# Attention with a gated feed-forward: x stored first and the gated tiles added to it in memory, first loads by SyncE, a new order of tasks

## The chip, the cores and the metric

The kernel runs on one core of a Trainium2 chip. The metric is device microseconds for one launch. A core has TensorE (PE in the profile, its weight loads PEld), VectorE (DVE), ScalarE (ACT), GpSimd (POOL) and SyncE (SP). Each runs its own list of instructions in order, and waits on semaphores for the others. Transfers are issued from SP's queue or from POOL's queue. All transfers share 16 DMA engines.

## The reference

Two stages follow one another. In the code below B is 4, H is 8, S is 768 and D is 64; heads 0, 2 and 6 attend to everything before them, the others only to the first 4 keys and to a window of 64.

```python
scores = scale * np.matmul(q, k.transpose(0, 1, 3, 2))
scores = np.where(mask, scores, -1e9)
a = np.exp(scores - max); a = a / (a.sum(-1) + 1e-9)
x = np.matmul(a, v).transpose(0, 2, 1, 3).reshape(3072, 512)

g, val = x @ w_gate, x @ w_val            # 512 -> 1536
ffn_out = (0.5 * g * (1 + erf(g / sqrt(2))) * val) @ w_out
out = x + sigmoid(x @ w_res) * ffn_out    # 3072 x 512, float32
```

## The kernel before

**Tiling.** The 3072 rows are cut into six chunks of 512 rows, four tiles of 128 each (`CHUNKS`, L25). The code numbers the chunks from 0; this text does too, so "from chunk 2 on" in the change's short name is `c >= 1`. For each chunk the kernel does attention, which leaves x for the 512 rows in `xtok` (128 x 4 x 512, f32, two buffers) and, transposed in f16, in `xT`; then `gate_value` (twelve blocks `f`, each with four matmuls of 512 columns for the gate and four for the value, a GELU on ACT and a product on DVE, L1166 and L1168); then the output.

**Output.** Chunk 0's first two tiles use plain matmuls (`output`, L1295). All other pairs of tiles use seven products in place of eight, on sums of halves (`output_fast`, L1212): `keep` copies a partial product out of PSUM, `plus` (L1257) adds another to it, `gated` (L1281) multiplies by `1 + tanh(res / 2)`, whose matmuls are `res`, and `add` (L1286) adds x from `xtok`. SP then stores the finished tile `otile` (128 x 512 f32, four buffers, L1292). For the last pair the adds go by half tiles, and each may go to DVE or POOL.

**Loads.** POOL issues all loads of queries, keys, values and weights (L577); each converts f32 in memory to f16 on the chip. Chunks 0 and 1 load rows of q and k and transpose them on PE (`loads_rows`, L709). Later chunks load tiles (`loads_natural`) and SP issues transposing transfers (L754) into `qkt`. For every batch, SP also copies one pair of heads of `qkt` to other partitions (`q6`, L762) and values shifted by half a tile (`vs`, L662). PE's score matmuls (L893) read `qkt` and `q6`; the weighted values (L516, L1017) read `va` and `vs`.

**Order.** `Graph.schedule` (L219) places every task once, at build time, on its engine's list. A task has a priority; the string `HINTS` (L46) overrides 171 of them by number. The planner's own estimates of each task (`c_act`, `c_dve`, and so on) decide which task is free next. What comes out is five fixed lists. Before the first gate block `g0` is placed, PE's idle time is filled with matmuls on zeros (`warm`, L1333). Each transfer has a semaphore, and SP's last instructions wait for all transfers named `out`.

**Shapes on PE.** A score matmul uses half of the rows of PE's array, the sink scores (L984) a quarter of the columns; the transposes and the window products use half of the columns; the rest uses the whole array, or from about chunk 3 on pairs of half-column matmuls (L517), so that less changes from one shape to the next.

Of the kernel before, what the change touches and what calls it, by code (L numbers as in the profile page):

```python
# [4 lines left out]
NHEAD = 8  # L5
# [15 lines left out]
AF = mybir.ActivationFunctionType  # L21
ALU = mybir.AluOpType
# [21 lines left out]


HINTS = (  # L46
    "3:-58.9 11:-130.04 428:854.14 430:718.61 444:2782.08 457:-821.9 460:407.45 490:4205.68 521:1522.06 "
    "591:-818.43 610:-36.63 612:486.89 613:-2965.25 619:1544.03 621:-44.07 643:467.87 644:-881 646:4.3 656:119.6 "
    "664:25.04 673:629.62 675:-109.25 695:-2674.26 696:-1856.67 703:-881.5 706:-108.75 707:714.39 708:1939.7 "
    "711:270.02 712:497.18 716:476.22 720:652.56 738:638.32 743:520.23 744:3053.24 749:514.3 750:1799.28 "  # L50
    "751:2383.53 756:521.28 762:1469.72 764:4344.87 767:2237.74 787:-603.93 815:5053.25 817:2978.67 821:1231.87 "
    "824:1484.86 836:2402.62 837:798.1 841:706.04 848:-288.52 849:2997.07 876:2751.74 906:2555.54 913:1516.93 "
    "918:2437.99 919:1519.88 924:1537.25 931:1510.23 936:2384.32 949:2443.79 955:2089.28 967:2846.74 995:-227.38 "
    "1001:29.83 1002:3171.86 1003:3180.29 1004:1146.58 1007:2686.58 1012:1781.89 1040:-803.29 1043:1907.45 "
    "1045:1028.83 1046:667.33 1050:3229.28 1051:1536.45 1053:3573.03 1056:-1823.77 1084:4090.27 1110:2454.97 "
    "1111:2597.62 1117:2808.38 1123:2507.5 1128:2481.58 1129:2529.63 1134:2508.5 1146:2434.73 1152:2779.33 "
    "1153:3034.61 1158:3861.94 1165:2795.06 1171:3076.63 1176:2997.8 1185:5989.69 1188:2243.92 1189:2528.84 "
    "1192:2789.39 1193:2537.45 1194:3836.22 1208:3021.15 1215:6294.68 1263:3219.13 1268:5037.38 1283:4420.5 "
    "1308:4756.92 1311:3513.6 1317:3517.03 1321:3052.3 1329:5930.49 1330:3507.5 1335:3508.5 1336:3519.22 "
    "1341:4624.14 1345:3444.6 1353:3516.64 1354:3538.83 1357:2761.66 1365:3787.63 1366:5173.04 1372:5102.72 "  # L60
    "1386:5438.32 1392:4014.31 1393:4933.66 1418:5146.68 1430:4133.91 1441:5428.8 1452:5127.54 1457:2188.42 "
    "1462:4595.33 1464:5711.23 1467:9389.54 1468:4425.54 ~1471:550.69 1476:5611.77 1499:4504.13 1513:6742.83 "
    "1516:5340.27 1522:4510.5 1523:4585.63 1526:3632.38 1534:4503.02 1539:4253.34 1550:4463.64 1565:7711.51 "
    "1570:4506.5 1571:5085.34 1580:2427.42 1594:2466.44 1610:9272.71 1625:3048.93 1627:6036.71 1629:6167.81 "
    "1631:5064.12 1644:6476.5 1662:4125.72 1671:5044.95 1672:7314.6 1676:4967.2 1683:6427.71 1692:9540.12 "
    "1711:7387.16 1757:5137.62 1784:5507.1 1797:5469.41 1803:7562.23 1817:7773.49 1818:7478.69 1823:7672.83 "
    "1834:7419.08 1836:10250.4 1849:7490.55 "
)

class Task:  # L70
# [118 lines left out]
SWAP = -3000.0  # L189
VK_AT = -18.5  # L190
VS_DMA = 0
LAT = {"pe": 0.20, "act": 0.10, "dve": 0.08, "pool": 0.12, "sp": 0.1}


class Graph:
# [205 lines left out]
    def emit(self):  # L401
        nc = self.nc
        sems = {e: nc.alloc_semaphore(f"cnt_{e}") for e in ENGS}
        val, groups = {}, {}
        for e in ENGS:
            n = 0
            for t in self.prog[e]:
                if t.dma:
                    key = (t.eng, t.grp) if t.grp is not None else t.seq
                    if key not in groups:  # L410
                        groups[key] = [nc.alloc_semaphore(f"dma_{t.seq}"), 0]
                    t.sem = groups[key][0]
                    groups[key][1] += 16
                    val[t] = key
                else:
                    n += 1 if t.signal else 0
                    t.sem = sems[e]
                    val[t] = n

        def run(name, engine):  # L420
            for t in self.prog[name]:
                for sem, v in dict.fromkeys((w.sem, groups[val[w]][1] if w.dma else val[w]) for w in t.waits):
                    engine.wait_ge(sem, v)
                self.run = t.run
                res = t.fn(engine)
                last = res[-1] if isinstance(res, (list, tuple)) else res
                if t.dma:
                    last.then_inc(t.sem, 16)
                elif t.signal:
                    last.then_inc(t.sem, 1)  # L430

        finals = [t for t in self.order_ if t.dma and t.name.startswith("out")]
        with nc.Block() as blk:

            @blk.gpsimd
            def _(e):
                run("pool", e)

            @blk.tensor
            def _(e):  # L440
                run("pe", e)

            @blk.scalar
            def _(e):
                run("act", e)

            @blk.vector
            def _(e):
                run("dve", e)

            @blk.sync
            def _(e):
                run("sp", e)
                for t in finals:
                    e.wait_ge(t.sem, 16)


def c_mm(n, k=1):
# [1 line left out]


def c_act(n):
    return 0.19 + n * 0.000834


def c_dve(n, rate=1.0, psum=True):
    return (0.125 if psum else 0.065) + n * 0.00104 / rate


def c_pool(n, rate=1.0):  # L470
# [3 lines left out]
def build_kernel(nc, q, k, v, w_gate, w_val, w_out, w_res, out):  # L474
    assert N_SINK <= 64 and WINDOW == 64
    G = Graph(nc)
# [195 lines left out]
    def loads_rows(c, si, b, a, z):  # L672

        n = z - a
        BB = batch(b)
# [11 lines left out]
        def piece(j, h, i):  # L687
            o = h * 256 if c == 0 else (j * NHEAD + h) * 128
            return at(st[j])[:, o + i * 64:o + (i + 1) * 64]
        for gi, (h0, h1) in enumerate(groups):  # L690
            for j, src in enumerate((q, k)):
                t = dma("pool", base + 4 * gi + j, (h1 - h0) * n * (0.092 if c else 0.089),
                        (lambda j=j, h0=h0, h1=h1: lambda: sv(j, h0, h1, n * 64))(),
                        src[b, h0:h1, lo:hi, :].rearrange("h (p j) d -> p h (j d)", j=n), bufs=[st[j]])
                t.late = 1.2 if c else 0.0
                for h in range(h0, h1):
                    tok[j, h] = t
        values(b, a, z, base + (10 if c == 0 else 2), False, c == 0)
# [33 lines left out]
    def loads_natural(c, si, b, a, z):  # L732
# [8 lines left out]
        for i in range(a, z):  # L741
            for j, src in ((1, k), (0, q)):
                st = sts[(i - a) // 2]

                def sv(i=i, j=j, st=st):
                    o = (j * 2 + (i - a) % 2) * 512
                    return at(st)[:, o:o + 512]
                ds = [dma("pool", base, 0.45,
                          (lambda sv=sv, o=o: lambda: sv().rearrange("p (o h d) -> p o h d", o=2, h=4)[:, o, :, :])(),
                          src[b, :, i * 128:(i + 1) * 128, :].rearrange("(h o) p d -> o p h d", o=2)[o], bufs=[st],  # L750
                          grp=("ld", b, i, j)) for o in range(2)]
                for d in ds:
                    d.late = 5.0
                t = G.add("sp", 1.65, (lambda sv=sv, i=i, j=j: lambda e: e.dma_start(  # L754
                    at(BB.qkt)[:, j, :, i * 128:(i + 1) * 128], sv(), transpose=True))(), ds, base, bufs=[st, BB.qkt], dma=0.85, name="dT")
                t.late = 1.0
                loaded.append(t)
                for p in range(NPAIR):
                    (BB.ktok if j else BB.qtok)[p, i] = t
            if i == a:  # L760
                values(b, a, z, base, False)
# [437 lines left out]
    def weight_sums():  # L1199
# [9 lines left out]
        add(2, w(1, 1), w(0, 1), tall)  # L1209
        add(3, w(1, 0), wt[:, 1], [t2])  # L1210

    def output_fast(c, pi, h, htoks, hs, stoks, xbuf, xtoks, xtbuf, xttoks):  # L1212
        segs = [(b, t) for (b, a, z) in CHUNKS[c] for t in range(a, z)]
        lts = (2 * pi, 2 * pi + 1)
# [57 lines left out]
        for i, lt in enumerate(lts):  # L1272
# [6 lines left out]
            for w, src, deps in parts:  # L1279
                n = w.stop - w.start  # L1280
                ends.append(G.add("dve", c_dve(n, 1.0, src is not None), (lambda w=w, src=src, ot=ot, sr=sr: lambda e: e.scalar_tensor_tensor(  # L1281
                    out=at(ot)[:, w], in0=at(sr)[:, w], scalar=1.0, in1=at(src or ot)[:, w], op0=ALU.add, op1=ALU.mult))(),
                    [tas[i]] + deps, pr + (len(ends) - 40 if end else 0), bufs=[sr, ot] + ([src] if src else []), name="gated"))
            adds = []
            for w, deps in [(p[0], [t_]) for p, t_ in zip(parts, ends)] if end else [(slice(0, 512), ends)]:
                fn = (lambda ot=ot, lt=lt, w=w: lambda e: e.tensor_tensor(  # L1286
# [57 lines left out]
    for c, segs in enumerate(CHUNKS):  # L1344
# [7 lines left out]
                xttoks.extend(halves[-1])  # L1352
        else:
            attention(c, segs, xbuf, xtbuf, xtoks, xttoks)
        h, htoks = gate_value(c, xtbuf, xttoks, halves)
        if c == 0:
            weight_sums()
# [87 lines left out]
```

The softmax here doesn't subtract the row's maximum and nothing guards it: scores larger than these inputs give would overflow.

## Time and profile before

| what | value |
|---|---|
| time, median of 3 runs (lowest to highest) | 266.18 us (265.86 to 267.08) |
| profiled execution, span | 263.7 us |
| median less span | 2.5 us |
| PE busy | 257.7 us, 98% of the span |
| DVE / ACT / POOL busy | 181.6 / 147.2 / 89.3 us |
| DVE adding x (L1286), full tiles | 21 instructions, 14.3 us in all |
| stores of output tiles (256 KB each) | 22, median 2.4 us from issue to landing |
| bytes read from / written to HBM | 29.36 / 6.29 MB |

The profiled execution's own time is its span; no other time is given for it. The span counts from the first to the last instruction of the program, and the 2.5 us are what lies around it.

In the profile, `out<-in` names what an instruction writes and reads, `xN` says how many like it are merged, and square brackets or the last columns give the engine's idle time before it and what ended that. The view of stretches gives, per stretch, its length and for each engine the busy time and the number of instructions. The chain of waits goes back from the last instruction to what released each step. For a transfer, "to landing" runs from its issue to the semaphore's last count.

### The profile page before, as it was taken

How to read it: one execution, taken by the hardware profiler on the slowest of the kernel's cores; microseconds unless marked ns; L12 is line 12 of the kernel's file. 1: busy time of each engine (PE TensorE's matmuls, PEld its weight loads, DVE VectorE, ACT ScalarE, POOL GpSimd, SP SyncE). 2: the span in 40 equal slices, each digit the busy share in tenths (PEclk: the TensorE clock that was granted, in tenths of full speed). 3: DMA queues.
4: the chain of work that ended last, by engine and by line, in shares of the span. 5: the costliest groups of instructions: out<-in, count | busy, mean ns of one | idle time of the engine just before them, and what ended most of it. 6: DMA issues, size and time to landing. Idle time of an engine off the chain costs nothing.

```text
span 263.7 us, 7495 instructions
## 1 busy us (share of the span) xinstructions
PE 257.7 (98%) x3226; PEld 164.0 (62%) x3226; DVE 181.6 (69%) x378; ACT 147.2 (56%) x237; POOL 89.3 (34%) x127
## 2 busy tenths in 40 slices
PE   7999999999999999999999999999999999999993
PEld 6777655468444668544567444589655588655692
DVE  2698437798447888557898366888557689837655
ACT  2785467974244987423787242967243888233430
POOL 8999979506109973975000000000000000000003
PEclk9999999999999999999999999999999999999999
DMA  6999999999999999999996110004200004200003
GB/s 83 174 204 206 188 175 231 175 153 204 134 200 148 165 137 177 171 179 176 174 156 150 42 40 0 2 26 101 82 2 0 2 2 122 82 2 0 2 35 127
DMA packets 96513, 29.22 MB, mean 111 GB/s; under 512 B 84449, under 2 KB 93025, under 8 KB 96481
## 3 DMA queue, kind: packets, MB, share of 16 engines
q0 software_dynamic: 70320, 14.69, 67.5%
q1 hardware_dynamic: 26160, 14.07, 28.0%
q8 instruction: 25, 0.41, 0.7%
q14 instruction: 8, 0.06, 0.1%
HBM read 29.36 MB, written 6.29 MB: 135 GB/s over the span
## 4 chain that ended last, share of the span: by engine, by line
PE 95%; DMA 2%; DVE 1%; issue 0%; POOLq 0%
PE ps L516 50%; PE ps L517 32%; PE ps L893 5%; PE ps L1333 2%; PE ps L1017 2%; PE ps L709 2%; DMA qks<-in_q_dram 2%; PE ps L1106 2%; PE ps L984 1%; DVE otile L1281 1%; DVE otile L1286 1%; DVE otile L1257 0%; POOLq L1427 0%
## 5 line engine op out<-in xcount | busy, mean ns | idle before, releaser
L1166 ACT ACTIVATE gact<-ps 128x512 f16<-128x512 f32 x68 | 40.2, 597 | 73.5 <-PE ps L516 43.7
L1168 DVE SCALAR_TENSOR_TENSOR hT<-gact,ps 128x512 f16<-128x512 f16 x68 | 46.1, 686 | 48.0 <-PE ps L516 23.1
L516 PE MATMUL ps<-xT,wg 128*128 128x512 f16 (+1 forms) x208 | 50.0, 363 | 0.0
L516 PE MATMUL ps<-xT,wv 128*128 128x512 f16 (+1 forms) x202 | 49.0, 362 | 0.0
L1286 POOL TENSOR_TENSOR otile<-otile,xtok 128x256 f32<-128x256 f32 x3 | 2.4, 801 | 136.2 <-DVE otile L1281 136.2
L577 POOL DMA_DIRECT2D qks<-in_k_dram x36 | 28.0, 810 | 17.3 <-DMA qkt<-qks 13.9
L516 PEld LDWEIGHTS ps<-xT,wg 128*128 128x128 f16 x208 | 20.1, 98 | 20.0 <-DVE otile L1257 0.3
L516 PEld LDWEIGHTS ps<-xT,wv 128*128 128x128 f16 x202 | 19.4, 98 | 20.0 <-DVE hT L1168 0.5
L577 POOL DMA_DIRECT2D qks<-in_q_dram x36 | 28.4, 828 | 2.2 <-issue 1.4
L517 PE MATMUL ps<-xT,wv 128*64 128x512 f16 x204 | 28.3, 380 | 0.0
L577 POOL DMA_DIRECT2D va<-in_v_dram x24 | 21.3, 920 | 15.1 <-PE ps L516 15.1
L517 PE MATMUL ps<-xT,wg 128*64 128x512 f16 x192 | 26.3, 379 | 0.0
L909 ACT ACTIVATE ea<-ps 128x1024 f16<-128x1024 f32 (+2 forms) x24 | 21.1, 915 | 1.7 <-PE ps L893 1.6
L1257 DVE TENSOR_TENSOR otile<-otile,ps 128x256 f32<-128x256 f32 x33 | 13.6, 417 | 7.1 <-PE ps L517 4.7
L1226 ACT ACTIVATE srs<-ps 128x512 f32<-128x512 f32 x22 | 13.1, 595 | 9.1 <-PE ps L517 6.7
L517 PEld LDWEIGHTS ps<-xT,wv 128*64 128x64 f16 x204 | 11.5, 110 | 9.8 <-DVE hT L1168 0.3
L1084 DVE TENSOR_TENSOR xtok<-ps,rcp 128x512 f32<-128x512 f32 (+1 forms) x28 | 16.8, 606 | 0.2
L517 PEld LDWEIGHTS ps<-xT,wg 128*64 128x64 f16 x192 | 11.1, 110 | 9.0
L893 PE MATMUL ps<-qkt 64*128 64x64 f16 (+4 forms) x391 | 16.4, 213 | 0.0
L893 PEld LDWEIGHTS ps<-qkt 64*128 64x128 f16 x391 | 9.8, 94 | 8.0 <-issue 4.2
L516 PE MATMUL ps<-wo,hT 128*128 128x256 f16 (+1 forms) x84 | 14.4, 304 | 0.0
L1286 DVE TENSOR_TENSOR otile<-otile,xtok 128x512 f32<-128x512 f32 (+1 forms) x21 | 14.3, 691 | 0.2
(109 smaller groups left out, 437.4 us busy)
## 6 DMA issues: line engine op xcount, KB each, us to landing
out_dram<-otile SPq DMA_DIRECT2D x22, 256.0 KB, 2.4
va<-in_v_dram POOLq DMA_DIRECT2D x24, 128.0 KB, 17.6
qks<-in_k_dram POOLq DMA_DIRECT2D x32, 64.0 KB, 12.6
qks<-in_q_dram POOLq DMA_DIRECT2D x32, 64.0 KB, 13.0
wg<-in_moe_w_gate_dram POOLq DMA_DIRECT2D x3, 512.0 KB, 10.2
wv<-in_moe_w_val_dram POOLq DMA_DIRECT2D x3, 512.0 KB, 12.1
wo<-in_moe_w_out_dram POOLq DMA_DIRECT2D x4, 384.0 KB, 22.8
vs<-va SPq DMA_DIRECT2D x4, 260.0 KB, 7.9
```

The source lines that it names most:

```text
L516: return e.matmul(o, lhsT=lhsT, rhs=rhs, **k)
L517: return [e.matmul(o[h:h + 64], lhsT=lhsT[:, h:h + 64], rhs=rhs, **k) for h in (0, 64)][-1]
L577: return G.add(eng, issue, lambda e: e.dma_start(out_ap(), in_ap), deps, prio, bufs=bufs, dma=cost, name=name, grp=grp)
L709: return [e.transpose(out=at16(scr)[64 * x:64 * x + 64, (m * n + i) * 128:(m * n + i + 1) * 128], in_=piece(jj, h, i), identity=ident[:, : ...
L893: return [e.matmul(at(scr)[:, oo:oo + w], lhsT=side(BB, low, 1)[half, k0:k0 + 128], rhs=side(BB, low, 0)[half, qq:qq + w], start=True, sto ...
L909: return e.activation(out=o, in_=i_, func=AF.Exp, scale=SM_SCALE)
L1084: t2 = G.add("dve", c_dve(2 * n * 64), lambda e: e.tensor_tensor(out=xview(), in0=avv(0, DHEAD), in1=scale(), op=ALU.mult), [t1] + xdeps, ...
L1166: ta = G.add("act", c_act(512), (lambda gb=gb, ga=ga: lambda e: e.activation(out=at(ga)[:, :], in_=at(gb)[:, :], func=AF.Gelu))(), [tg], p ...
L1168: th = G.add("dve", c_dve(512), (lambda vb=vb, ga=ga, f=f: lambda e: e.scalar_tensor_tensor(out=hv(f), in0=at(ga)[:, :], scalar=0.5, in1=a ...
L1226: tas.append(G.add("act", c_act(512), (lambda rb=rb, sr=sr: lambda e: e.activation(out=at(sr)[:, :], in_=at(rb)[:, :], func=AF.Tanh, scale ...
L1257: return G.add("dve", c_dve(256), lambda e: e.tensor_tensor(out=dst(), in0=dst(), in1=at(D)[:, 0:256], op=ALU.add), [t, k], pr, bufs=[D, o ...
L1286: fn = (lambda ot=ot, lt=lt, w=w: lambda e: e.tensor_tensor(out=at(ot)[:, w], in0=at(ot)[:, w], in1=at(xbuf)[:, lt, w], op=ALU.add))()
```

## The change

Five things change.

1. For chunks 1 to 5 a new task `xst` on SP stores x from `xtok` to the output rows as soon as attention has made it (for the last chunk only the first two tiles). The `add` on DVE and the store on SP go away for those tiles. After `gated`, POOL issues a transfer of `otile` to the output with an accumulating addition; it waits for the landing of `xst`. The last pair of tiles stays as it was.
2. Chunk 0's queries and keys of heads 0 to 3 are loaded by SP in four transfers as f32 into a free `xtok` buffer; four `cast` tasks (DVE or ACT) make f16 of them. Heads 4 to 7 still come by POOL.
3. The planner's estimates `c_act` and `c_dve` are changed.
4. `HINTS` is new as a whole (259 entries), so all five lists are new.
5. The two transposing transfers of a tile (q and k) share a semaphore, and the final wait takes the group's count.

```diff
+ACCUM = 1
@@ emit
                 for t in finals:
-                    e.wait_ge(t.sem, 16)
+                    e.wait_ge(t.sem, groups[val[t]][1])
@@ planner's estimates
 def c_act(n):
-    return 0.19 + n * 0.000834
+    return 0.17 + n * 0.000834
 def c_dve(n, rate=1.0, psum=True):
-    return (0.125 if psum else 0.065) + n * 0.00104 / rate
+    return 0.15 + n * 0.00105 / (2.0 if rate > 1.0 else 1.0)
@@ loads_rows
-        for gi, (h0, h1) in enumerate(groups):
+        if c == 0:
+            f32 = Buf(P_x)
+            for m in range(2):
+                for j, src in ((1, k), (0, q)):
+                    dst = (lambda m=m, j=j: at(f32)[:, 2 * m + j, :].rearrange("p (h w) -> p h w", h=2))
+                    t = G.add("sp", 0.65, (lambda dst=dst, src=src, m=m: lambda e: e.dma_start(
+                        dst(), src[b, m:m + 3:2, lo:hi, :].rearrange("h (p j) d -> p h (j d)", j=n)))(), [], -200 + 2 * m + 1 - j,
+                        bufs=[f32], dma=0.01, name="ld32")
...
+                    t = G.flex({"dve": (c_dve(512, 1.0, False), cast("dve")), "act": (c_act(512), cast("act"))}, [t],
+                               -700 + 2 * m + 1 - j, bufs=[f32, st[j]], name="cast")
+                    tok[j, m] = tok[j, m + 2] = t
+        for gi, (h0, h1) in list(enumerate(groups))[c == 0:]:
@@ loads_natural
-                    ..., bufs=[st, BB.qkt], dma=0.85, name="dT")
+                    ..., bufs=[st, BB.qkt], dma=0.85, name="dT", grp=("dT", b, i))
@@ output
+    stored = {}
+
+    def store_x(c, xbuf, xtoks):
+        n = 2 if c == len(CHUNKS) - 1 else 4
+        r0 = c * 512
+        stored[c] = G.add("sp", 0.65, lambda e: e.dma_start(
+            out[r0:r0 + n * 128, :].rearrange("(i p) d -> p i d", p=128), at(xbuf)[:, 0:n, :]),
+            list(dict.fromkeys(t for i in range(n) for t in xtoks[i])), 1000 * c - 3500, bufs=[xbuf], dma=0.65 * n, name="xst")
+        stored[c].late = 1.0
...
+            if c >= ACCUM and not end:
+                t = G.add("pool", 1.0, (lambda ot=ot, r0=r0: lambda e: e.dma_start(out[r0:r0 + 128, :], at(ot)[:, :], accum_op=ALU.add))(),
+                          ends + [stored[c]], pr - 3000, bufs=[ot], dma=1.0, name="out")
+                t.late = 0.5
+                continue
@@ main loop
             attention(c, segs, xbuf, xtbuf, xtoks, xttoks)
+        if c >= ACCUM:
+            store_x(c, xbuf, xtoks)
```

## The prediction

> **What bounds the kernel now.** I read the stretches first, then the start, the end, and two landings. Stretches (length, then busy time and instructions of PE, PEld, DVE, ACT, POOL, PE's clock, DMA share, GB/s):
>
> ```profile
> 0.00:24.90 24.90, 23.13 (x402) 19.12 (x403) 16.68 (x54) 15.61 (x32) 23.64 (x42) 1.00 1.27 165
> 24.90:257.40 232.50, 232.46 (x2798) 143.34 (x2797) 161.24 (x318) 130.98 (x205) 63.97 (x84) 1.00 0.95 105
> 257.40:263.70 6.30, 2.11 (x32) 1.53 (x28) 3.66 (x8) 0.60 (x1) 1.71 (x3) 0.99 0.35 125
> ```
>
> From 24.9 to 257.4 PE is never idle: 232.46 of 232.50. Nothing can be won there but PE's own work; a late transfer can lose there. What can be shortened is the start and the 6.3 us of the end. The start, from the timeline (start, length, engine, line):
>
> ```profile
> 1.06 3.93 PE L1333 MATMUL ps<-blank 128*128 128x128 f16 x41 [1.06 <-DVE blank L549]
> 1.32 0.91 POOL L577 DMA_DIRECT2D qks<-in_q_dram  x1 [0.80 <-POOLq L1427]
> 3.19 0.31 POOL L535 TENSOR_SCALAR_AFFINE_SELECT ident<-ident 128x128 f16<-128x128 f16 x1
> 5.68 0.64 PE L709 MATMUL ps<-ident,qks 128*64 128x128 f16 x16 [0.69 <-DMA qks<-in_q_dram]
> 8.25 0.48 PEld L893 LDWEIGHTS ps<-qkt 64*128 64x128 f16 x20
> 8.64 0.81 ACT L909 ACTIVATE ea<-ps 128x768 f16<-128x768 f32 x1 [0.56 <-PE ps L893]
> 19.72 1.03 PE L516 MATMUL ps<-xT,wg 128*128 128x256 f16 x8
> ```
>
> The first loads land at 5.7 (q) and 7.0 (k); the first exponential starts at 8.64, the first gate matmul at 19.72. Between, PE fills with 124 warm matmuls. The end, from the chain of waits:
>
> ```profile
> 259.33 1.01 DVE otile L1281 x3
> 260.34 0.02 issue
> 260.37 0.77 DVE otile L1286
> ```
>
> The last `gated` ends at 260.3, the last add at 261.1; its store is issued at 261.16 and lands 2.0 later. Last, chunk 2's `q6` copy and the first matmul that reads it:
>
> ```profile
> 80.98 0.67 SPq L762 DMA_DIRECT2D q<-qkt  x1
> 90.03 0.38 PE L893 MATMUL ps<-q 64*128 64x384 f16 x2
> ```
>
> The copy lands at 88.56, 1.5 us before its use, in a stretch in which the page's DMA digits stand at 9.
>
> **What the Trainium skill says.** DMA: Bandwidth & Descriptors, SWDGE vs HWDGE vs iDMA: only GpSimd can issue an accumulating transfer. So the chunk stores must move from SP's queue to POOL's; no trace here shows one. Same page, Issuing engines are not separate DMA queues: SP's and POOL's transfers run on the same 16 engines and interleave. The trace agrees: `vs` copies of 65 KB take 5.2 to 5.8 us to land at 37 to 45 us, output tiles of 256 KB only 2.0 once the loads are over. Collectives: The Full Stack, The bandwidth ceiling: a reducing transfer reads two sources per chunk and moves at about half rate; not shown here. TensorEngine Tiling (Array Packing), Key Properties: changing the tiling mode drains the array. The trace agrees: eight half-column matmuls of 512 columns take 0.87 us from start to start before their like (206.00 to 206.87) and 0.97 before a score group (209.09 to 210.06), 0.10 a change.
>
> **The change part by part.** Sums are against the 263.7 us span; the median lies 2.5 above it.
>
> *DVE's adds.* Eighteen full adds go, 18 x 0.69 = 12.4 us of DVE. Worth nothing inside: PE runs over the whole of it without a gap. Only an add at the end counts.
>
> *The end.* The new order ends as the old one: last `gated`, a half tile of chunk 5's second tile, read from PSUM, about 0.8 after PE's last matmul. Then 0.77 (add) and 2.0 (store) = 2.8 go, and a POOL transfer comes, with nothing behind which to hide. Its issue costs 0.74 to 0.97 on POOL (all rows of L577). POOL's first load took 4.3 to land with nothing before it, of which some 1.3 are its own data (the second landed 1.3 later). An output tile's 256 KB land in 2.0 by SP. So from below 3.0 (that 2.0 with POOL's issue of 0.9 in place of SP's 0.33, and the reading of the old row), from above 5.4 (the first load plus half its data again and a slower add). I take 3.9: +1.1, range +0.2 to +2.6. POOL's last half-tile add (0.84) stands before it but is over by then.
>
> *The start.* SP's four loads (256 KB each) start about 0.9, and land from 3.1 to 6.3 if each takes about 0.8 to 1.1, shared with POOL's q of heads 4 to 7. ACT then has four casts (0.60 each, its row of 512) in time that was idle. But `ident` now stands behind four loads on POOL: 1.32 + 0.91 + 2 x 0.91 + 0.75 = 4.8, +0.31 = 5.1. First transposes at about 5.2, against 5.68; first exponential about 7.7 against 8.64. From there to the gates ACT is nearly full: its list to the table load sums to 9.6 us (before 10.0 in 10.8). In the new order PE has 98 warm matmuls after the first transposes, before 83: 15 x 0.056 = 0.8 us more filler. So 0.5 won at the head of PE and 0.8 given back before the gates; and w_val's first piece now is issued behind four v tiles, two other weight pieces and w_out's last: by the landings' spacing (weights 2.5, w_out 1.9, v 1.05, q or k 1.4) it lands at about 22, where PE reaches it between 21.5 and 23. I take +0.1, range -1.0 to +1.2.
>
> *PE's order.* In all 110 stretches of one shape in place of 115, after the start three fewer: -0.3.
>
> *Transfers in the middle.* Loads ahead of chunk 1's values: seven tile loads (0.57 each) and SP's 1 MB come before them, the two loads replaced go. The last v tile lands at 51 to 52.5 (before, the same queue was through with w_out at 50.4), its `vs` copy 5.3 to 6 later, 57 to 58.5. PE reaches the window product that waits for it at 56.4 + one `res` moved before it (0.85) = 57.3. Wait: 0 to 1.2.
> Chunk 2: on SP, `q6` now stands behind `xst` and a last transpose. Chunk 0's stores hold SP until about 66.5 as before (66.99); then four transposes of 1.3 to 3.3 each, a store, and `xst`, at about 74; its 1 MB is four output tiles of 0.9 (spacing of two landings at 75.5 and 76.4), 3.5 us. The last transpose lands at 84 to 88 (lags 7 to 10), `q6` is issued then, and needs 7.6: 92 to 95. PE, two score groups and two products later than before, wants it at 92. Wait: 0 to 3.5; I take 1.6 for both waits together, since they are one backlog. PE's in-order list stands behind the waiting score group, products included, so nothing covers it.
>
> *Priced at nothing.* Accumulates on POOL hold 23 q and k loads behind them until about 97 to 105; those loads were issued by 121.2 and are first wanted at 165 and 204. Four `otile` buffers: chunks lie 40 us apart. The shared semaphores and the final wait: no work.
>
> Sum: +1.1 + 0.1 - 0.3 + 1.6 = +2.5; I shade the backlog to 1.1, as its lower end is zero: +2.0, span 265.7, time **268.2**.
>
> **The rivals.** *No wait in the middle.* If `q6` lands by 92, only end, start and shapes remain: +0.9, **267.1**, no change. For: the stretch before had not one wait, with margins like 1.5. Against: xst is a new 1 MB in the full queue.
> *Faster through the start.* The keys arrive 2.5 us earlier, ACT starts 0.9 earlier. If the filler and the weights don't give it back, the gates start at 18.0 to 18.5 (-1.5), shapes -0.3, the end +0.2 at its lower bound: -1.6, **264.6**. It decides once the first 256-column gate matmul is before 18.4 and PE stays closed. Against it: the 15 fillers more.
> *DVE was the hidden limit.* Then 12.4 us less of DVE would show as several us, **262**. Against: PE's waits for DVE sum to about 1 us.
> *Accumulates don't overlap with SP's queue*, or add at a quarter of the rate: a backlog of 5 us and an end of +2.6, **271**.
>
> **How the numbers follow.** Wait in the middle 0.43, with the slow accumulates 0.05; no wait 0.24; faster start 0.24; DVE 0.04. What a measurement of this kernel can tell from no change is about 0.5%, 1.3 us: below 264.85 is faster, above 267.5 slower. Faster 0.28, same 0.24, slower 0.48. The range leaves out the DVE case and the worst backlog: 263.8 to 271.0. The likeliest case's own range is 266.8 to 271.
>
> **What would show it.** Right: a gap on PE between 88 and 96 that ends with `q<-qkt` or a transpose, or one near 57 on `vs`; the first gate matmul at 19 to 20; the last accumulate 3.5 to 4.5 from the last `gated` to its landing. Wrong: PE closed from 25 to the end; gates before 18.4; an accumulate landing in 2.5; gaps before `out` on POOL that hold loads past 160.

## The result, and the profile after

The changed kernel takes **278.78 us** (277.32 to 280.64, four runs), beside 266.02 us (265.63 to 267.08) for the kernel before on the same chip: ratio **1.048**, 95% interval 1.043 to 1.054. That is slower, as the forecast's sign had it, but 10.6 us over the forecast of 268.2 and outside its range, 263.8 to 271.0. The ratios in this document leave out an execution that is over 1.5% above the fastest of its kernel (one each of `fill` and `end_add` below), the medians keep it. The profiled execution, the slowest of the four (280.64 us), has a span of 278.6, before 263.7: +14.9, where the medians differ by 12.8.

From the page of the kernel after: its span, and the clock that was granted to PE in 40 slices of 7 us, in tenths of full speed.

```profile
span 278.6 us, 7528 instructions
...
PEclk9599999999999999999979999999999999999996
```

Before, the recorded clock was at full speed throughout. Now it falls to half in the second slice and to 0.7 in the one from 139 on, and both slices hold a place where PE had nothing to do (the last slice is the end). The view of stretches of the kernel after, in the same columns as before (length; busy time and instructions of PE, PEld, DVE, ACT, POOL; PE's clock; DMA share; GB/s), first for the three stretches of the prediction, then for the two slow places:

```profile
0.00:24.27 24.27, 20.08 (x335) 16.25 (x335) 12.26 (x40) 15.99 (x28) 22.74 (x41) 0.86 1.30 183
24.27:268.30 244.03, 239.46 (x2891) 154.09 (x2890) 158.72 (x322) 133.50 (x208) 77.25 (x98) 0.99 1.06 120
268.30:278.60 10.30, 2.55 (x39) 1.87 (x34) 2.68 (x6) 0.60 (x1) 3.17 (x4) 0.77 0.49 76
```

```profile
8.60:12.00 3.40, 3.40 (x48) 2.44 (x48) 1.38 (x2) 2.30 (x4) 3.24 (x8) 0.50 1.88 180
...
141.10:145.00 3.90, 3.90 (x52) 2.56 (x50) 1.23 (x4) 1.85 (x3) 0.54 (x1) 0.61 1.75 175
```

The middle is no longer closed: PE lacks 4.6 us of it. PE is fully "busy" from 8.6 to 12.0, but with matmuls that take twice their time. The start, from the timeline:

```profile
1.83 0.98 SPq L707 DMA_DIRECT2D xtok<-in_q_dram  x2
...
7.87 0.63 ACT L715 ACTIVATE qks<-xtok 128x512 f16<-128x512 f32 x1 [2.83 <-DMA xtok<-in_q_dram]
...
8.55 0.64 PE L739 MATMUL ps<-ident,qks 128*64 128x128 f16 x8 [2.37 <-ACT qks L715]
...
11.31 0.81 ACT L939 ACTIVATE ea<-ps 128x768 f16<-128x768 f32 x1 [0.69 <-PE ps L923]
...
24.27 0.93 PE L527 MATMUL ps<-xT,wg 128*128 128x256 f16 x7
```

The keys land at 3.70 and 4.39, but the queries, issued right behind them, only at 7.85 and 9.23. PE has three warm matmuls for that time and then waits 2.37. The first exponential is at 11.31 (before 8.64), the first gate matmul at 24.27 (before 19.72). Now chunk 2, where the prediction looked for its wait, and then chunk 3, from the same view (SyncE's issues, then PE):

```profile
82.23 0.58 SPq L1247 DMA_DIRECT2D out_dram<-xtok  x1
82.85 1.74 SPq L784 DMA_TRANSPOSE qkt<-qks  x1
...
90.66 0.67 SPq L792 DMA_DIRECT2D q<-qkt  x1
...
130.89 1.19 SPq L784 DMA_TRANSPOSE qkt<-qks  x1
...
134.37 0.63 SPq L792 DMA_DIRECT2D q<-qkt  x1
...
141.00 0.93 PE L923 MATMUL ps<-qkt 64*128 64x64 f16 x13 [2.45 <-DMA q<-qkt]
```

The store of x (L1247, 1 MB) goes ahead of chunk 2's last transposing transfer, which lands at 90.52; PE waited 0.45 for it here. The second `q6` (L792) is chunk 3's. It is issued at 134.37, lands at 140.95, and PE has waited 2.45 for it. A transposing transfer ahead of it was held until 130.89. And the end, from the chain of waits:

```profile
269.96 0.21 issue
270.16 0.88 POOL out_dram L1325
271.04 0.76 POOL otile L1331
271.80 0.81 POOLq L444
```

The last two accumulates are issued at 270.16 and 271.61 and land at 274.18 and 276.73; the span ends 1.8 us after that. The last `gated` and the last accumulate, from the timeline:

```profile
270.89 0.42 DVE L1321 SCALAR_TENSOR_TENSOR otile<-srs,ps 128x256 f32<-128x256 f32 x1
271.61 1.00 POOL L1325 DMA_DIRECT2D out_dram<-otile  x1
```

The first gate matmul of each chunk makes a milestone that all these kernels have. The table has the lengths between some of them in us, from the profiled executions; its last column is an experiment below. (The expectations of runs 3 and 6 call the third one chunk 4's; it is chunk 3's, at 144.68 before and 155.75 after.)

| stretch | before | after | difference | `all_undone` |
|---|---|---|---|---|
| start to first gate matmul, chunk 0 | 19.72 | 24.27 | +4.55 | 21.73 |
| on to chunk 1's | 45.09 | 46.44 | +1.35 | 46.51 |
| on to chunk 3's | 79.87 | 85.04 | +5.17 | 81.02 |
| on to PE's last matmul | 114.82 | 115.10 | +0.28 | 113.71 |
| on to the end of the span | 4.20 | 7.75 | +3.55 | 4.13 |
| sum | 263.70 | 278.60 | +14.9 | 267.10 |

### The profile page after: what moved, and what is told of

It is laid out like the page before. It is cut to its first block, busy times and chain, and to the rows that moved or that the text cites. A ratio compares the mean times of both kernels' runs of the same rounds, so it can differ in the third digit from the quotient of the medians.

```text
span 278.6 us, 7528 instructions
## 1 busy us (share of the span) xinstructions
PE 262.1 (94%) x3256; PEld 172.2 (62%) x3256; DVE 173.7 (62%) x366; ACT 150.1 (54%) x236; POOL 103.2 (37%) x142
## 4 chain that ended last, share of the span: by engine, by line
PE 73%; DMA 13%; SPq 5%; POOL 3%; DVE 2%; issue 1%; POOLq 0%; ACT 0%; DVEq 0%
PE ps L528 31%; PE ps L527 29%; DMA qks<-in_q_dram 6%; PE ps L923 5%; SPq L784 3%; DMA qkt<-qks 3%; PE ps L1378 3%; DMA q<-qkt 2%; DMA xtok<-in_q_dram 2%; PE ps L1047 2%; PE ps L739 2%; POOL va L588 2%; PE ps L1136 1%; SPq L673 1%; DVE otile L1321 1%
## 5 line engine op out<-in xcount | busy, mean ns | idle before, releaser
L1325 POOL DMA_DIRECT2D out_dram<-otile x18 | 16.0, 917 | 94.6 <-DVE otile L1321 65.1
L527 PE MATMUL ps<-xT,wv 128*128 128x512 f16 (+1 forms) x198 | 48.3, 362 | 0.0
L528 PE MATMUL ps<-xT,wv 128*64 128x512 f16 x212 | 29.8, 379 | 0.0
L528 PE MATMUL ps<-xT,wg 128*64 128x512 f16 x200 | 28.4, 379 | 0.0
L588 POOL DMA_DIRECT2D va<-in_v_dram x24 | 22.1, 942 | 13.9 <-PE ps L1047 12.6
L528 PEld LDWEIGHTS ps<-xT,wv 128*64 128x64 f16 x212 | 14.3, 110 | 8.2 <-issue 0.3
L923 PE MATMUL ps<-qkt 64*128 64x64 f16 (+3 forms) x391 | 17.0, 220 | 2.4 <-DMA q<-qkt 2.4
L528 PEld LDWEIGHTS ps<-xT,wg 128*64 128x64 f16 x200 | 13.7, 110 | 7.2 <-DVE hT L1198 0.3
L939 ACT ACTIVATE eb<-ps 128x1024 f16<-128x1024 f32 (+3 forms) x16 | 13.2, 857 | 3.4 <-PE ps L923 3.3
L528 PE MATMUL ps<-wr,xT 128*64 128x512 f16 x120 | 14.7, 380 | 0.0
## 6 DMA issues: line engine op xcount, KB each, us to landing
wg<-in_moe_w_gate_dram POOLq DMA_DIRECT2D x3, 512.0 KB, 13.7
wv<-in_moe_w_val_dram POOLq DMA_DIRECT2D x3, 512.0 KB, 12.8
```

Of the source, the lines that this page charges most:

```text
L527: return e.matmul(o, lhsT=lhsT, rhs=rhs, **k)
L528: return [e.matmul(o[h:h + 64], lhsT=lhsT[:, h:h + 64], rhs=rhs, **k) for h in (0, 64)][-1]
L588: return G.add(eng, issue, lambda e: e.dma_start(out_ap(), in_ap), deps, prio, bufs=bufs, dma=cost, name=name, grp=grp)
L923: return [e.matmul(at(scr)[:, oo:oo + w], lhsT=side(BB, low, 1)[half, k0:k0 + 128], rhs=side(BB, low, 0)[half, qq:qq + w], start=True, sto ...
L939: return e.activation(out=o, in_=i_, func=AF.Exp, scale=SM_SCALE)
L1325: t = G.add("pool", 1.0, (lambda ot=ot, r0=r0: lambda e: e.dma_start(out[r0:r0 + 128, :], at(ot)[:, :], accum_op=ALU.add))(), ends + [stor ...
```

## The experiments

The changed kernel's five lists (in runs 10 to 12 those of the kernel before) were kept as the planner made them; each experiment then moves or replaces single tasks in the finished lists and assigns the waits anew, so that nothing else is planned differently. Lines are those of the changed kernel, in runs 10 to 12 nearly those of the kernel before. Single executions of the changed kernel and its relatives differ by up to 5.3 us, those of the kernel before by under 3; the last section says what the profiles show on that. The medians of runs 1 to 3 are 1.3 to 2.3 us below the changed kernel's, which is within that spread and not clear of noise: what those runs show is in their profiles.

From the profile I made three theories. **S**: the start is late since the f32 queries share the engines with GpSimd's loads, and PE's idle time halves its clock. **Q**: `q6` is late by its place in SyncE's queue. **E**: the accumulate at the end is slow. The rivals: the new order itself costs the time, whoever loads; or the engines are overfull from the stores of x and the accumulates, whatever the places. After runs 1 to 4 a fourth came up, **T**: from 55 to 141 the transfers set the time, so that PE's gains are waited for at the next late one.

**1. The start undone (`start_pool`).**

```diff
-SP:   k(m=1) k(m=0) q(m=0) q(m=1) as f32; ACT: four casts
-POOL: q 4-7, v, v, k 4-7, ident, v, ...
+POOL: k 0-3, q 0-3, ident, q 4-7, k 4-7, v, v, v, ...
```

> The changed kernel with its start undone: no f32 loads by SyncE and no casts; keys and queries of heads 0 to 3 are the first two loads of GpSimd's queue again, then those of heads 4 to 7, then v; the order on PE, DVE and everything later is that of the changed kernel. Theory S (the queries land at 7.85 and 9.23 because both halves share the engines with GpSimd's loads; PE has three fillers for the time and is idle for 2.37 us, after which its clock is granted at half until about 14): PE closed from 5.7 on, clock 1.00, first exponential at 8.6 to 9.0, first gate matmul at 19.5 to 20.5 instead of 24.3, time 274 to 275. Rival (the new order itself costs the time, whoever loads): first gate matmul not before 23, time 277.5 or more. Between: if the queue of transfers sets chunk 1 anyway, the gate matmul comes 4 us earlier but up to 3 us come back as a wait for the vs copy near 57 to 62, time 276 to 278.

Measured: 277.48 us, ratio 1.044 (1.038 to 1.051). First gate matmul at 23.26, one us earlier, not four. The loads land at 5.67 and 6.98 as before, yet PE runs at half speed until 13.0: the new order has few warm matmuls between its first transposes, and run 8, with 32 more, has full speed there. And the time came back: a wait of 2.08 at 91.06, with half speed after it. Theory S in its simple form fails.

**2. The gap filled (`fill`).**

```diff
-qkT qkT warm x3 qkT
+qkT qkT warm x43 qkT
```

> The changed kernel with 40 more warm matmuls on PE in the gap before the second transposes (6.2 to 8.5), nothing else. The queries still land at 7.85 and 9.23, so the wait itself stays. If the half clock from 8.6 to 14 follows from PE's idle time: clock 1.00 throughout the start, first gate matmul 2 to 3 us earlier (21.5 to 22.5), time 276 to 277. If the clock falls for another reason: still 0.50 near 9 to 12, time 278.8 or, as the fillers could overrun, up to 279.5.

Measured: 276.80 us, ratio 1.038 (1.032 to 1.045). The first line is the timeline of the changed kernel, the second that of this run, for the same eight warm matmuls:

```profile
12.20 1.03 PE L1378 MATMUL ps<-blank 128*128 128x128 f16 x8
```

```profile
11.23 0.62 PE L1378 MATMUL ps<-blank 128*128 128x128 f16 x8
```

The queries land as late as in the changed kernel, and PE is at full speed when they are there; first gate matmul at 22.61. So about 1.7 of the 4.55 at the start was half speed; in four other profiles with the start as changed the gates came at 23.64 to 24.06, so it can be as little as 1.0. But chunk 1's first gate matmul stood at 70.64, against 70.71: PE now waited 2.19 at 63 for a `vs` copy (landed at 62.99), and 3.28 at 93.5 for a transposed tile (landed at 93.28).

**3. One place on SyncE (`q6_ahead`).**

```diff
-SP: dT dT(chunk 5) vs vs q6(chunk 3)
+SP: dT q6(chunk 3) dT(chunk 5) vs vs
```

> The changed kernel with one instruction moved: on SyncE the copy q6 of chunk 3 goes ahead of two vs copies and of the transposing transfer that stood before it and waited until 130.9 for a load that GpSimd had issued among accumulates. Theory Q (that place in SyncE's queue made q6 late): q6 issued near 124 instead of 134.4, landing at 131 to 135; no wait of PE for q6 at 138.5, clock 1.00 there, chunk 4's first gate matmul 4 to 5 us earlier, time 273.5 to 275. Rival (the transfer engines are simply overfull from xst and the accumulates): q6 lands little earlier, or PE waits about as long for a vs copy or another transposed tile just after; time 277 to 279.

Measured: 276.44 us, ratio 1.040 (1.032 to 1.047). `q6` is issued at 124.27 and lands at 129.56; PE passes 138 without a wait. The profiled execution ends at 273.9, 4.7 earlier, as theory Q has it. The median gained only 2.3, with executions from 274.51 to 278.17. The profiled one waits only 0.26 at 91, where five of its relatives with `xst` in the same place wait 1.2 to 5.4; what its other executions had there no profile shows.

**4. The end undone (`end_add`).**

```diff
-gated; POOL: out += otile         (two tiles of chunk 5; x stored before)
+gated; DVE: otile += x; SP: out = otile
```

> The changed kernel with its end undone: for the two tiles of chunk 5 that it accumulates, DVE adds x and SyncE stores the sum, and the store of x for these two tiles goes; all else as changed. Theory E (the last accumulating transfer takes 5.1 us to land and 1.9 more to the end, where add and store took 2.8): the time from PE's last matmul to the end falls from 7.7 to about 4, time 274.5 to 275.5. As I had forecast it (accumulate 3.9 against 2.8): gain of 1.1, time 277.7.

Measured: 274.38 us, ratio 1.028 (1.020 to 1.036). From PE's last matmul to the end 4.1 us instead of 7.75. Theory E holds.

**5. PE made earlier once more (`fill_v`).**

```diff
 PE:   as in fill
-POOL: v2 w v3 k w q v4         (v: chunk 1's v tiles, w: chunk 2's)
+POOL: v2 v3 v4 w k w q
```

> The changed kernel with the 40 warm matmuls in the start's gap, and on GpSimd's queue two of chunk 1's four v tiles moved ahead of five other loads; nothing else. Theory T (from 55 to 141 the transfers set the time, so what PE wins earlier is waited for at the next late transfer): the last vs copy lands near 59 instead of 63, PE reaches the window product at 60 to 61 and no longer waits there (fill alone: 2.19), chunk 1's first gate matmul 68 to 68.7 instead of 70.6; but PE then comes 2 us earlier to the transposed tiles near 91 and waits 3 to 5 there, time 275.5 to 277, hardly under fill alone. Rival (the later transfers move up with it): no wait over 2 near 91, time 274 to 275.

Measured: 279.41 us, ratio 1.051 (1.048 to 1.053): slower than `fill`, and no faster than the changed kernel. The last `vs` copy lands at 59.49 in place of 63.05, PE does not wait for it, and chunk 1's first gate matmul is at 68.16, 2.5 earlier. Then comes, from the timeline and the stretches of this run:

```profile
93.18 0.72 PE L1014 MATMUL ps<-qkt 64*32 64x512 f16 x8 [5.41 <-DMA qkt<-qks]
```

```profile
93.20:98.20 5.00, 5.00 (x19) 1.74 (x20) 2.52 (x7) 1.01 (x2) 4.73 (x7) 0.50 1.63 114
```

What PE had won was waited for, and the longer wait was followed by 5.0 us at half speed (the 0.50 in the second line), which the shorter one in `fill` was not. Chunk 2's first gate matmul: 116.85, against 111.94 in the changed kernel. Theory T's direction is right, its price was too low.

**6. Both places on SyncE (`queue`).**

```diff
-SP: xst(chunk 1) dT q6(chunk 2) ... dT dT(chunk 5) vs vs q6(chunk 3)
+SP: dT q6(chunk 2) xst(chunk 1) ... dT q6(chunk 3) dT(chunk 5) vs vs
```

> The changed kernel with two places on SyncE changed: chunk 3's q6 as in the run q6_ahead, and the first store of x (1 MB, chunk 1) behind chunk 2's last transposing transfer and its q6, which it stood ahead of; nothing else. Theory T, by places in the queue: the last transposed tile of chunk 2 lands 2 to 3 us earlier (87 to 88.5), no wait over 0.6 near 91 and none at 138 to 141; from chunk 1's first gate matmul to chunk 4's 80 to 81.5 us (before 79.9, changed 85.0), time 274 to 275. Rival (the engines are overfull, whatever the places): waits of 2 and more stay or move to the next transfer, that stretch 83.5 or more, time 276.5 or more.

Measured: 274.54 us (273.76 to 274.64), ratio 1.032 (1.029 to 1.034). From its stretches:

```profile
63.00:92.00 29.00, 29.00 (x224) 16.12 (x219) 19.22 (x37) 14.42 (x24) 11.13 (x14) 1.00 1.53 177
92.00:138.00 46.00, 46.00 (x481) 27.64 (x478) 30.63 (x66) 29.28 (x44) 32.14 (x43) 1.00 1.79 161
```

PE is closed again. The last transposed tile of chunk 2 lands at 87.46 in place of 90.52, and from chunk 1's first gate matmul to chunk 3's it takes 80.55 (changed 85.04, before 79.87). The four executions lie within 0.9 us of each other. The stores of x and the accumulates are all still there, so their traffic alone is not the cause of the waits in this stretch. The time that is still lost lies mostly ahead of chunk 1's gates and at the end.

**7. Plain writes (`no_rmw`).**

```diff
-e.dma_start(out[r0:r0 + 128, :], at(ot)[:, :], accum_op=ALU.add)
+e.dma_start(out[r0:r0 + 128, :], at(ot)[:, :])
```

> The changed kernel with its 18 accumulating transfers as plain writes from the same queue at the same places (leaves out the addition of x in those 18 tiles). If the reading and adding in memory makes the load of the engines: GpSimd's loads issued at 112 to 116 land in 8 to 11 us instead of 11 to 16, no wait of PE near 141, last transfer lands in about 3 us; time 274 to 276. If it is only what stands ahead of what in the queues: the waits near 91 or 141 stay at 2 to 3.5 us in sum, only the end becomes 1 to 2 shorter; time 277 to 278.

Measured: 274.47 us, ratio 1.031 (1.026 to 1.037). The accumulates' group on the page (busy, mean ns of one), first of the changed kernel, then of this run:

```profile
L1325 POOL DMA_DIRECT2D out_dram<-otile x18 | 16.0, 917 | 94.6 <-DVE otile L1321 65.1
```

```profile
L1325 POOL DMA_DIRECT2D out_dram<-otile x18 | 10.2, 567 | 95.3 <-DVE otile L1321 65.0
```

This kernel leaves x out of those 18 tiles. The adding makes the issue 0.35 dearer. At the end, where the queues are quiet, the plain writes land in 2.3 and 2.5 us, the adding ones in 4.0 and 5.1; at 113 to 119 it is 9.7 and 8.1 against 11.6 and 13.7. SyncE's transposing transfer was held less long (its load landed at 124.69 in place of 130.87), `q6` was issued at 127.27, and PE did not wait for it; a wait of 1.20 at 90.7 stayed. So the late `q6` needs both: the place, and adding transfers that delay the load that the transfer in front of it waits for. Either one removed was enough, in one profile each.

**8. Five things undone together (`all_undone`).** The edits of 1, 4, 5 (the v tiles) and 6, and 32 more warm matmuls in three gaps of the start.

> The changed kernel with five things undone together: the start's loads (GpSimd, no f32, no casts) with 32 more warm matmuls in its gaps, the two v tiles of chunk 1, the two places on SyncE, and the end (DVE adds, SyncE stores for chunk 5's two tiles). It keeps the 16 accumulating transfers and stores of x of chunks 1 to 4 and the new order on PE, ACT and DVE. If these five account for the loss: first gate matmul at 21 to 21.8, no wait of PE over 0.6 between 25 and its end, clock 1.00, span 264.5 to 267, time 267 to 269.5. If the new order or the accumulates cost by themselves: time 271 or more, with PE's matmuls longer without any wait, or with waits in other places.

Measured: 269.56 us (268.92 to 270.44), ratio 1.015 (1.012 to 1.018). Its stretches:

```profile
0.00:21.73 21.73, 19.44 (x366) 16.42 (x367) 12.60 (x40) 13.48 (x24) 20.17 (x38) 1.00 1.28 157
21.73:260.40 238.67, 237.47 (x2891) 150.68 (x2890) 158.46 (x322) 133.53 (x208) 81.70 (x103) 1.00 1.09 122
260.40:267.10 6.70, 2.57 (x40) 1.90 (x34) 3.92 (x8) 0.60 (x1) 1.57 (x2) 0.99 0.33 120
```

The clock is 1.00, the span 267.1: 11.5 of the 14.9 us are back (in the medians, 9.2 of 12.8). The remaining 3.4 are all ahead of chunk 1's gates (2.0 and 1.4 in the table): from there to PE's last matmul it takes 194.73, before 194.69. Sixteen accumulates and four stores of x are in that stretch, and 16 adds of DVE are not; with the new order of PE they come to nothing in sum. It is a sum of +1.15 up to chunk 3's gates and -1.11 behind them, and what the order and the accumulates are worth by themselves no run shows.

**9. The first scores first (`all_scores`).** As 8, with the transposes of queries 4 to 7 behind the first scores.

> The run all_undone with one thing more: the transposes of the queries of heads 4 to 7, which the new order has ahead of the first scores, go behind them on PE, as do their copies on ACT and DVE. If they are what holds the start: first exponential 0.7 to 1.2 us earlier, first gate matmul at 20.6 to 21.2 instead of 21.7, and 268 to 269 us instead of 269.6. If not: gates at 21.5 to 22, time 269.3 to 270.

Measured: 269.64 us, ratio 1.015 (1.012 to 1.017). The first exponential came at 8.98 in place of 10.11, the first gate matmul at 21.85: a miss. What the new order loses ahead of the gates lies in what follows, and was not taken apart further.

**10. The f32 loads alone, in the order before (`before_f32`), and 11. with GpSimd held back (`before_held`).**

```diff
-POOL: q 0-3, k 0-3, masks, q 4-7, k 4-7, ...
+SP: q(m=0) q(m=1) k(m=0) k(m=1) as f32; ACT: four casts
+POOL: two masks, q 4-7, k 4-7, ...              (before_f32)
+POOL: all masks, q 4-7, k 4-7, v, v, v, v, ...  (before_held)
```

> The kernel before with the f32 loads alone: SyncE loads queries and keys of heads 0 to 3 as f32 (queries first, as PE's order there wants them), ACT casts them; GpSimd starts with the loads of heads 4 to 7; nothing else moved. If the loads collide as in the changed kernel: the last two pieces land at 7.5 to 9.3, first scores at 9.5 to 10.3 instead of 8.26, PE at half speed for some us, first gate matmul 21.5 to 23.5 instead of 19.7, time 267.5 to 269.5. If it is the new order of tasks that makes them late: first scores by 8.3, time 265 to 266.3.

> As before_f32, but GpSimd makes all its masks first (some 2.7 us) and only then starts to load, so that the f32 pieces have the engines for themselves. They then land by 5.5 to 6.5, first scores at 7.4 to 7.9, first gate matmul 18.8 to 19.8, time 264.5 to 266. If heads 4 to 7 and v are then what is late: first gate matmul after 20.5, time 266.5 to 267.5.

Measured: 270.51 us, ratio 1.016 (1.014 to 1.019), and 266.36 us, ratio 1.003 (1.001 to 1.004). In `before_f32` the second pair of pieces lands at 7.11 and 9.03, beside GpSimd's loads at 9.35 and 10.66. PE's timeline there:

```profile
10.22 0.64 PE L709 MATMUL ps<-ident,qks 128*64 128x128 f16 x16 [4.01 <-ACT qkt L723]
10.79 1.25 PE L1333 MATMUL ps<-blank 128*128 128x128 f16 x10
11.98 1.14 PE L893 MATMUL ps<-qkt 64*128 64x128 f16 x20
```

The ten warm matmuls took 0.73 before, the twenty scores 0.70. First gate matmul at 24.19, 4.5 late; at PE's last matmul it is still 4.1. Held back, the pieces land at 3.53, 4.19, 5.69 and 6.37; with its cast the last is ready at 7.02, while the two f16 loads of the kernel before were ready at 6.94. So the f32 way wins nothing even undisturbed.

**12. The accumulation alone, in the order before (`before_acc`).**

```diff
-DVE: gated, add; SP: out = otile            (chunks 1 to 4)
+SP: xst at the place of the chunk's first store
+DVE: gated; POOL: out += otile, all 16 behind the last load
```

> The kernel before with the accumulation alone: for chunks 1 to 4 SyncE stores x (1 MB each, where the chunk's first output tile was stored) and GpSimd adds the 16 gated tiles in memory, all queued behind its last load; 15 DVE adds and 16 stores go; start, end and every other order are those of before. Theory P (the accumulates cost by their place in the queues and at the end, not by themselves, and DVE's adds were worth nothing): the same as before within 0.5 per cent, 264.7 to 266.9, PE closed from 25 to its end. Rival (stores of x and reading in memory overfill the engines): a wait of over 1 us on q6, vs or a transposed tile between 96 and 150, 267.5 or more. Rival (DVE was a hidden limit): 264 or less.

Measured: 276.53 us, ratio 1.041 (1.039 to 1.044): theory P as I had placed it fails. From the timeline of this run:

```profile
123.93 3.67 POOL L1293 DMA_DIRECT2D out_dram<-otile  x4
...
140.14 0.42 DVE L1251 COPY otile<-ps 128x256 f32<-128x256 f32 x1 [10.40 <-DMA out_dram<-otile]
...
140.62 0.61 PE L516 MATMUL ps<-wt,hS 128*128 128x256 f16 x2 [9.55 <-DVE otile L1251]
```

Behind the last load in GpSimd's queue, chunk 1's four accumulates needed 16 to 19 us to land, and all that time they held the four output buffers. Chunk 2's first partial product had nowhere to go: PE waited 9.55 and then ran at half speed until 147. This tests my placement of the accumulates, not the accumulation itself; run 8 comes nearest to that.

## Why the prediction was wrong, point by point

*The start* (+0.1, range to +1.2; measured +4.55). The failing step is "land from 3.1 to 6.3 if each takes about 0.8 to 1.1, shared with POOL's q". The keys did (3.70, 4.39); the queries came 3.5 and 1.4 us apart, because GpSimd's loads were being moved at the same time: in the order before, the second pair lands at 7.11 and 9.03 beside them and at 5.69 and 6.37 without (runs 10 and 11). I had just written that both queues interleave on the same engines, and counted one of GpSimd's loads where four were issued by 4.1 us. The f32 loads alone cost all of it in the order before (run 10). In the new order they are one cause among others: without them, and at full speed, 2.0 of the 4.55 stay (run 8), and why is not shown. Whether the added warm matmuls (by the profiles 101 after the first transposes begin, before 83) cost their 0.8 us no run tests. The first transposes came at 5.27, as I had said.

*Half speed*. No step had it. The sum added waits as if a wait cost its own length. Run 2 shows some 1.0 to 1.7 us from it at the start, and from run 5 I estimate that a wait of 5.41 costs 2.5 more behind it (5.0 us at half speed). The Trainium skill has the mechanism, in TensorE: Matmul & The Clock Gate, What's actually happening: PE's clock is halved after an idle window of about 3.4 us, and comes back after as long a busy one. These traces agree on the length of the window, 3.41 us, but not that all of it must be idle: 2.08 us were enough (last section). I had not drawn on that page, since PE had no such wait before.

*Chunk 1's values* (v tile at 51 to 52.5, `vs` at 57 to 58.5; measured 55.73 and 63.05). Mis-sized: GpSimd's loads ran some 3 us later than I had put them, here as at the start (the w_val piece put at about 22 landed at 24.71); why is not shown. The `vs` copy then took 7.3 us in place of 5.3 to 6. The wait itself was only 0.60 in the profile, because PE was late too. The cost was covered, not absent: run 2, with PE 1.66 earlier, waited 2.19 there.

*Chunk 2* (last transposing transfer 84 to 88, a wait of 0 to 3.5 on `q6` or a transposed tile near 92). The mechanism is right: with the 1 MB of `xst` ahead of it the last transposed tile landed at 90.52 (90.4 to 93.3 in seven profiles), and putting `xst` behind gave 87.46 (run 6). In the profile above the wait is 0.45, in five others with `xst` in that place 1.2 to 5.4. That `q6` landed at 93.80, inside my 92 to 95, is luck: chunk 0's stores held SyncE until 73.76, not 66.5, `xst` went out at 82.23, not at 74, and then `q6` took 3.1 us, not 7.6. PE wanted it only at 98.10.

*Priced at nothing: the accumulates that hold loads*. "First wanted at 165 and 204" is the step whose reasoning failed. PE does not want the loads' data earlier, but SyncE's queue is in order: a transposing transfer for chunk 5 waited for one of them (issued at 115.13, landed at 130.87), and chunk 3's `q6`, wanted at 138.5, stood behind it. I asked who reads the data, and not who queues behind the reader. It cost some 4 us of the profiled span (from chunk 1's gates to chunk 3's 80.87 in run 3, in place of 85.04); the median of run 3 gained only 2.3.

*The end* (+1.1, range +0.2 to +2.6; measured +3.55). Mis-sized twice. From the last `gated` to the landing it took 5.4 us, 5.1 of them after the issue, where I took 3.9: the sum had one accumulate, and the last one goes out 1.45 behind another that is still on its way (that one landed in 4.0). And 1.8 us, not 0.5, lie between the last landing and the end of the span when GpSimd issued it. With `gated` ending 0.4 sooner after PE's last matmul, 2.6 + 1.3 - 0.4 makes the 3.5.

*PE's order* (-0.3): not seen by itself; from chunk 3's gates to PE's last matmul it takes 115.10, before 114.82.

*DVE's adds* (worth nothing) and *the four output buffers* (nothing): in keeping with run 8, where no gain from the missing adds and no wait for a buffer shows; run 12 shows that the buffers are free only while the accumulates land quickly.

*The rivals*. The worst one, a backlog of 5 us in the middle and 2.6 at the end, was nearest and had a chance of 0.05; it lacked the start and half speed. In my sum start, middle and end each stood with a small size, and no rival let all three be large. That the waits in the middle are one backlog was right: a transfer that is late early on makes PE late, which hides the next late transfer.

## What to carry to other kernels

When a transfer is added to an in-order queue, ask of each transfer behind it not when its data are read, but which other queue waits for it and what stands behind that wait. A wait of PE of 2 us or more can be charged twice, once as a wait and once as half speed behind it. Dummy matmuls in such a gap kept the speed up (run 2), though what they won was waited for later. An earlier stage made faster is worth nothing, or less, if it only lengthens the wait at the next late transfer. Accumulating in memory takes work from an engine that may not be the limit, and puts a slower transfer in its place; as the last transfer of a kernel it has nothing behind which to hide.

## What the runs showed of the hardware

Half speed comes in windows that do not start with a wait. In the changed kernel the recorded clock falls at 7.60, 140.72 and 273.84: twice 133.12 us, or 39 times 3.413. In each of the other profiles with several falls they also lie whole multiples of 3.41 apart, and up to PE's last matmul half speed in the record lasts 3.41, 6.83 or 13.65 us at a time. Cut into such windows, all fourteen profiles show one pattern. Where the recorded clock was full and PE was idle for 2.08 us or more of a window, the clock fell at the window's end; where PE was idle for up to 1.96, it did not. The first two lines are `start_pool`, the other three `fill` (length; PE's busy time and matmuls; clock; DMA share; GB/s):

```profile
88.16:91.58 3.42, 1.34 (x13) 1.00 2.68 90
91.58:94.99 3.41, 3.41 (x9) 0.50 1.61 120
```

```profile
88.79:92.20 3.41, 1.45 (x7) 1.00 3.65 184
92.20:95.61 3.41, 2.08 (x16) 1.00 2.03 130
95.61:99.02 3.41, 3.41 (x41) 1.00 1.39 88
```

The wait of 2.08 lies inside one window and was followed by half speed; the wait of 3.28 is split into 1.96 and 1.33 and was not. The windows of `fill` are counted back from the fall of its recorded clock at 273.11, which is 53 windows after 92.20. So the length of a wait does not decide alone: waits of 1.91, 2.08, 2.15, 2.37, 2.42, 2.45, 4.01, 5.41 and 9.55 us were followed by half speed, 2.19 and 3.28 were not, and of those up to 1.3 us in the middle none was. It may also be why single executions differ: a landing a few tenths later, or windows that lie otherwise, can decide over 2 or 3 us. No run varied the idle time alone, so the limit of about 2 us is read from these profiles and not tested.

At the start PE ran at half speed while the record of the granted clock said 1.00: in `start_pool` the eight warm matmuls at 11.41 took 1.03 us, as in the changed kernel, where the record said 0.50. The lengths of like matmuls are the surer witness. The Trainium skill's same page (TensorE: Matmul & The Clock Gate, Seeing it yourself) warns that the record is not to be trusted fully; these runs agree.

An accumulating transfer of 256 KB takes 0.92 us of GpSimd to issue and, with the queues quiet at the end, 3.8 to 5.1 us to land; a plain one from the same queue 0.57 and 2.3 to 2.5; a plain one from SyncE 0.33 and 2.0. The end of the span comes 1.8 us after the last landing in the seven profiles where GpSimd issued it, and 0.5 to 0.7 in the seven where SyncE did.
